# Batching the value products of a fused attention and MLP-mixer kernel: three eT tiles, two e tiles, one place for queries and keys

## The chip, the core and the metric

The kernel runs on one core of one Trainium2 chip. The metric is the device time of one execution in microseconds (us). The kernel before takes 1402.13 us, the median of three runs that lie between 1402.13 and 1402.17 us. One further execution was recorded by the hardware profiler; its span, from the first to the last instruction, is 1401.9 us, and all views below are of that execution.

Engines are named as in the profile: PE is the matrix engine (PEld its weight loads), DVE the vector engine, ACT the scalar engine, POOL the GpSimd engine, SP the engine whose queue issues most transfers. "L463" is line 463 of the kernel before.

## What is computed

```python
# q, k, v: (8, 8, 576, 64) float32; tau a scalar; the four weights arrive as float64
scores = (q @ k.T) / 8                         # per batch row and head, 576 x 576
thresh = scores.max(-1) - tau
scores = where(scores >= thresh, scores, -1e9)
attn   = softmax(scores)
x      = concat_heads(attn @ v)                # (8, 576, 512)

h   = relu(x.T @ w_tok1) @ w_tok2              # tokens are mixed: 576 -> 256 -> 576
u   = x + h.T
out = u + relu(u @ w_ch1) @ w_ch2              # channels are mixed: 512 -> 1536 -> 512
```

Everything is float32 on the chip. The weights are float64 in memory; they are loaded as pairs of 32-bit words and turned into float32 by integer and float operations on DVE, ACT and POOL, spread over the first units of the kernel.

## The kernel before

The attention is cut into 144 units, 18 for each of the eight batch rows (b = 0 to 7). A unit is 128 queries of two heads against all 576 keys. Nine units serve two pairs of heads: four blocks of the first pair, one shared block (`"s"`, the last 64 queries of both pairs), and four blocks of the second. The main loop does, for each unit `u`: the score products of `u`, the softmax normalization of `u-1`, the transposition of the weights of `u-2`, and the exponentials of `u`. Between these it slips in steps of the MLP of the batch row before, taken from the queue `todo` by `fill`; this filler is most of the PE work. At the end of the unit come the value products (`values`) that are due.

```python
LAG = 2
for u in range(len(units) + LAG + 4):
    ...
    scores(u)
    norm(u - 1)
    if b_now: weight(2)                  # steps of the conversion of the weights
    turn_blocks(u - LAG)                 # row b=0: turn(), with transposes on PE
    # when a group is complete: due += [(u + 2, ...)]  (u + 1 in row b=0)
    if b_now: fill(0.4)
    weight(2 if b_now else 1)
    weigh(u)
    if b_now: fill(0.6)
    weight(2 if b_now else 1)
    if t < 8: load_qk(n + 2 + t // 4, ..., t % 4)      # a quarter of a pair's q and k
    if t == 2: prep(n + 1)               # DVE transposes q and k, the loaded tiles are free again
    if t == 7: prep(n + 2)
    # while due: values(b, p, c); after the last group of a row: push(b)
```

A PE score product writes two PSUM tiles (`sc`, one per head). DVE takes the maxima, POOL makes a bias of them, and ACT writes `e` from `sc` (L316), which frees the PSUM tiles, and then takes the exponentials in place (L319):

```python
def scores(u):                            # cut
    sc = [(ps_3rd if b == 0 and (2 * u + h) % 3 == 2 else ps_sc).tile(...) for h in range(2)]   # ps_sc: two tiles
    nc.tensor.matmul(sc[h][rows, f, 0:HS], lhsT=qT[r, cols], rhs=kT[r, HS * f : HS * f + HS], ...)    # L301
    nc.vector.tensor_reduce(out=mx[:, c], in_=sc[h][:, :, 0:HS], axis=AX.XY, op=ALU.max)              # L306
    nc.gpsimd.tensor_scalar(out=bias[:, c], in0=mx[:, c], ...)                                        # L307

def weigh(u):
    e = work.tile([P, 2 * S], F32, tag="e", bufs=3, name=f"e_{u}")
    for h in range(2):                                                                               # L316
        nc.scalar.activation(out=eh, in_=sc[h][:, :, 0:HS], func=AF.Prelu, bias=bias[:, h : h + 1], ...)
    for h in range(2):                                                                               # L319
        nc.scalar.activation(out=eh, in_=eh, func=AF.Exp, bias=ntau, accum_out=rs[:, h : h + 1])
```

From row b=1 on, `e` is transposed in 32 x 32 blocks by DVE into `T` (L363), and 16 transfers from the SP queue (L373) put the blocks of a finished group in their places in `eT`. In row b=0 PE transposes `e` in three thirds, each into a PSUM tile of the pool `ps_tr` (two tiles), from which DVE or ACT copies it into `eT` (L352, L354):

```python
def turn_blocks(u):                       # cut; u here is two units back
    nc.vector.transpose(out=T..., in_=e...)                               # L363
    if place == n - 1:                    # the group is complete
        eTs[key] = work.tile([P, NK * 2 * P], F32, tag="eT", ...)         # two eT tiles
        for a in range(4):
            for i in range(4):
                nc.sync.dma_start(out=eTs[key][...], in_=T[...])          # L373
```

`values` multiplies one group (256 queries of one pair, or 64 of the shared block) with v. It uses one `ps_tr` tile, and ACT copies the result out (L413):

```python
def values(b, p, c):                      # cut
    ps = ps_tr.tile([P, MAIN], F32, tag="tr", name=f"pv_{b}_{p}_{c}")[:, 0:N]
    # 2 matmuls on vl (L403), 8 on lv (L408), two heads side by side in the PE columns
    nc.scalar.copy(out=x, in_=ps)         # L413
```

The filler consists of `turn_x` (L425), `tok1` (L434, ACT applies the relu), `tok2` (L441, DVE adds the result to xT, L445), `ch1` (L463, ACT applies the relu, L464) and `ch2` (L475 and L479, DVE copies the result, L484). All but `turn_x` use the two PSUM tiles of `ps_mm`. `push(b)` refills the queue when the attention of row b is done, three units into the next row, and sets how much filler a unit gets:

```python
KEEP = 45.0
def push(b):
    steps, old = token_mlp(b), list(todo)          # 5 turn_x, 2 tok1, 8 tok2
    todo.clear()
    for i in range(max(len(steps), len(old))):     # old and new steps in turn
        todo.extend(old[i : i + 1]); todo.extend(steps[i : i + 1])
    for i in ...: todo.extend(channel_mlp(b - b % 2, uT, i))
    quota = (sum(c for c, _ in todo) - (KEEP if b else 0.0)) / (UB - 1)     # UB = 18
```

Of the kernel before, what the change touches and what calls it, by code (L numbers as in the profile page):

```python
# [9 lines left out]
F32 = mybir.dt.float32  # L10
# [7 lines left out]
P = 128  # L18
# [3 lines left out]
def kernel(  # L22
# [26 lines left out]
    nc = tc.nc  # L49
    B, H, S, D = q.shape  # L50
# [7 lines left out]
    NT = NI + 1  # L58
    MT = [P] * NI + [LAST]
    NP = H // 2  # L60
    NTK = DTOK // P
# [3 lines left out]
    NK = 2 * S // P  # L65
# [4 lines left out]
    ld = ctx.enter_context(tc.tile_pool(name="ld", bufs=2))  # L70
    work = ctx.enter_context(tc.tile_pool(name="work", bufs=2))
# [11 lines left out]
    pairs = [(b, p) for b in range(B) for p in range(NP)]  # L83
# [3 lines left out]
    UB = 9 * NP // 2  # L87
# [5 lines left out]
    loaded = {}  # L93
    VL = 4
    vlast = [const.tile([P, P], F32, name=f"vl{i}") for i in range(VL)]

    def load_qk(n, eng, part=None):


        b, p = pairs[n]  # L100
        if n not in loaded:
            loaded[n] = [ld.tile([P, S // 32, 32], F32, tag=tag, name=f"{tag}_{n}") for tag in ("lq", "lk")]
        for i in range(4) if part is None else (part,):
            h, c = divmod(i, 2)
            for src, t, on in zip((q, k), loaded[n], eng):
                on.dma_start(
                    out=t[32 * i : 32 * i + 32], in_=src[b, 2 * p + h, :, 32 * c : 32 * c + 32].rearrange("(n t) d -> t n d", t=32)
                )

    def load_v(n):  # L110

        b, p = pairs[n]
        lv = ld.tile([P, NK, D], F32, tag="lv", bufs=4, name=f"lv_{n}")
        nc.sync.dma_start(out=lv, in_=v[b].rearrange("h s d -> (h s) d")[2 * S * p : 2 * S * p + 2 * S, :].rearrange("(c p) d -> p c d", p=P))
        vals[n] = lv
# [51 lines left out]
    def load_piece(i):  # L167
        if i >= len(pieces):
            return
        dst, src = pieces[i]  # L170
        rows = dst.shape[0]
        n = 1
        for d in dst.shape[1:]:
            n *= d
        raw = raw_at[i % NRAW][0:rows, 0 : n * (2 if wide(i) else 1)].bitcast(src.dtype)
        nc.sync.dma_start(out=like(raw, dst), in_=src)
        if wide(i):
            words = raw.bitcast(U32).rearrange("p (n w) -> p n w", w=2)
            h2 = work.tile([P, WMAX], F32, tag="o", name=f"h2_{i}")[0:rows, 0:n]
            raws[i] = like(words[:, :, 0], dst), like(words[:, :, 1], dst), like(h2, dst)  # L180
        else:
            raws[i] = like(raw, dst)
# [56 lines left out]
        weight(3 * i + 4 - steps_done)  # L239

    load_piece(0)
    load_qk(1, (nc.sync, nc.sync))
    load_v(0)
    for i in range(1, NRAW):
        load_piece(i)
# [26 lines left out]
    eTs = {}  # L272
    Ts = {}

    def in_blocks(b):
        return b > 0

    def prep(n):
        lq, lk = loaded.pop(n)
        made = []  # L280
        for src, name in ((lq, "qT"), (lk, "kT")):
            sb = work.tile([P, S], F32, tag=name, name=f"{name}_{n}")
            nc.vector.transpose(out=sb, in_=src.rearrange("p n d -> p (n d)"))
            made.append(sb)
        heads[n] = made
# [24 lines left out]
    def weigh(u):  # L310
        sc, bias = st.pop(u)
        rs = small.tile([P, 2], F32, tag="rs", name=f"rs_{u}")
        e = work.tile([P, 2 * S], F32, tag="e", bufs=3, name=f"e_{u}")
        for h in range(2):
            eh = e[:, S * h : S * h + S].rearrange("p (f x) -> p f x", f=2)
            nc.scalar.activation(out=eh, in_=sc[h][:, :, 0:HS], func=AF.Prelu, bias=bias[:, h : h + 1], scale=SCALE, alpha=STEEP)  # L316
        for h in range(2):
            eh = e[:, S * h : S * h + S]
            nc.scalar.activation(out=eh, in_=eh, func=AF.Exp, bias=ntau, accum_out=rs[:, h : h + 1])  # L319
        st[u] = e, rs  # L320
# [11 lines left out]
    def group_of(u):  # L332

        b, p0, t = units[u]
        if t == SHARED:
            return (b, p0, "s"), 0, 1
        i, c = divmod(t - (t > SHARED), NI)
        return (b, p0 + i, c // 2), c % 2, 2

    def turn(u, third):  # L340

        key, place, n = group_of(u)
        e = st[u]
        if third == 0 and place == 0:
            eTs[key] = work.tile([P, NK * 2 * P], F32, tag="eT", name=f"eT_{u}")
        if third == 2:
            st.pop(u)
        eT = eTs[key][:, 0 : NK * n * P].rearrange("p (c x) -> p c x", c=NK)
        ps = ps_tr.tile([P, MAIN], F32, tag="tr", name=f"tr{third}_{u}")[:, 0 : 3 * P].rearrange("p (c x) -> p c x", c=3)
        for c in range(3):  # L350
            k0 = (3 * third + c) * P
            nc.tensor.transpose(out=ps[:, c, :], in_=e[:, k0 : k0 + P], identity=ident)  # L352
        on = nc.scalar.copy if third == 1 and u % 2 else nc.vector.tensor_copy
        on(out=eT[:, 3 * third : 3 * third + 3, P * place : P * place + P], in_=ps)  # L354

    def turn_blocks(u):

        key, place, n = group_of(u)
        e = st.pop(u)
        if place == 0:  # L360
            Ts[key] = work.tile([P, NK * 2 * P], F32, tag="T", name=f"T_{u}")
        T = Ts[key][:, 0 : NK * n * P]
        nc.vector.transpose(  # L363
            out=T.rearrange("p (a c n x) -> p c a n x", a=4, c=NK, n=n)[:, :, :, place, :],
            in_=e.rearrange("p (c a x) -> p c a x", c=NK, a=4),
        )
        if place == n - 1:
            del Ts[key]
            eTs[key] = work.tile([P, NK * 2 * P], F32, tag="eT", name=f"eT_{u}")
            w = NK * n * 32  # L370
            for a in range(4):
                for i in range(4):
                    nc.sync.dma_start(  # L373
                        out=eTs[key][32 * a : 32 * a + 32, w * i : w * i + w], in_=T[32 * i : 32 * i + 32, w * a : w * a + w]
                    )
# [116 lines left out]


    KEEP = 45.0
    todo = deque()
    quota = 0.0
    credit = 0.0
# [11 lines left out]
    def push(b):  # L509
        nonlocal quota  # L510
        uT = xTs[b]
        steps, old = token_mlp(b), list(todo)
        todo.clear()
        for i in range(max(len(steps), len(old))):
            todo.extend(old[i : i + 1])
            todo.extend(steps[i : i + 1])
        for i in range(2) if b % 2 == 0 else range(2, (2 * S + GR - 1) // GR):
            todo.extend(channel_mlp(b - b % 2, uT, i))
        quota = (sum(c for c, _ in todo) - (KEEP if b else 0.0)) / (UB - 1)

    prep(0)
    due = deque()
    b_now = 0
    LAG = 2
    for u in range(len(units) + LAG + 4):
        on = u < len(units)
        if u == UB:
            late.close()
            ps_mm = ctx.enter_context(tc.tile_pool(name="ps_mm", bufs=2, space=bass.MemoryType.PSUM))
        if on:  # L530
            b_now, p0, t = units[u]
            n = b_now * NP + p0
        w = u - LAG
        back = 0 <= w < len(units)
        if on:
            scores(u)
        if 0 < u <= len(units):
            norm(u - 1)
        if b_now:
            weight(2)  # L540
        if back:
            key, place, many = group_of(w)
            if in_blocks(key[0]):
                turn_blocks(w)
            else:
                for i in range(3):
                    turn(w, i)
            if place == many - 1:
                b, p, c = key
                if c == 0 and p % 2 == 0:  # L550
                    split_middle(b * NP + p)
                if c == "s":
                    split_middle(b * NP + p + 1)
                when = u + (2 if in_blocks(b) else 1)
                due += [(when, b, p + i, c) for i in range(2 if c == "s" else 1)]
        if b_now:
            fill(0.4)
        weight(2 if b_now else 1)
        if on:
            weigh(u)  # L560
        if b_now:
            fill(0.6)
        weight(2 if b_now else 1)
        if on:
            m = n + 2 + t // 4
            if t < 8 and m < len(pairs):
                load_qk(m, (nc.scalar if b_now else nc.sync,) * 2, t % 4)
                if t % 4 == 3:
                    load_v(m)
            if t == 2:  # L570
                prep(n + 1)
            if t == 7 and n + 2 < len(pairs):
                prep(n + 2)
        while due and due[0][0] <= u:
            _, b, p, c = due.popleft()
            values(b, p, c)
            if p == NP - 1 and c == 1:
                push(b)
    need(len(pieces) - 1)
    quota = 1e9  # L580
# [29 lines left out]
```

## The time and the profile before

| what | value |
| --- | --- |
| median time of three runs | 1402.13 us |
| span of the profiled execution | 1401.9 us |
| DVE busy | 585.6 us (42%) |
| ACT busy | 589.1 us (42%) |
| POOL busy | 359.1 us (26%) |
| score products L301, x1280 | 192.3 us |
| value products L403 and L408, x1920 | 200.2 us |
| ch1 L463, x1920 | 401.7 us |
| ch2 L479, x864 | 388.9 us |
| transposes T on DVE, L363, x126 | 1369 ns each |
| first e operation on ACT, L316, x288 | 740 ns each |

The page gives for every engine how long it was busy, and a strip that cuts the span into 40 equal slices with one digit each: the busy share in tenths. The strip PEclk gives the granted clock of PE in the same slices. Groups of instructions are given by line, with the mean duration of one. In the timeline view a row is a run of equal instructions: its start, its length, the engine, the line, output and input, and, in brackets, how long the engine had been idle before it and which engine's work ended that idle time. PE's durations overlap a little, because a matmul's reported end is modelled; a start minus the start before it is the safer measure. The value row of the table is the sum of four groups (127.0, 43.6, 19.6 and 10.0 us).

### The profile page before, as it was taken

What the parts mean: (1) busy time and instruction counts of PE and PEld (TensorE: products, weight loads), DVE (VectorE), ACT (ScalarE), POOL (GpSimd) and SP (SyncE); (2) the same over time, 40 slices, a digit from 0 to 9 for tenths busy, and PEclk for the clock granted to TensorE, in tenths of its full rate; (3) what the DMA queues carried; (4) which work ended last, traced back from release to release, by engine and by line L of the source; (5) the groups of instructions that cost most, each with busy time, mean ns of one, the idle gap of its engine ahead of it and who ended that gap; (6) DMA issues with size and microseconds to landing.
All of it is one profiled execution on the core that took longest, in us unless ns stands there. A gap on an engine that the chain in (4) does not pass through costs nothing.

```text
span 1401.9 us, 19510 instructions
## 1 busy us (share of the span) xinstructions
PE 1332.0 (95%) x6866; PEld 833.3 (59%) x6866; DVE 585.6 (42%) x1009; ACT 589.1 (42%) x1328; POOL 359.1 (26%) x683
## 2 busy tenths in 40 slices
PE   5776899989999999999999999999999999999998
PEld 3443566646665567565656566565657566576675
DVE  5689674445444443434333444434333444201000
ACT  5676564444545444453334444443334444220110
POOL 4466462222222222212122222222212222100000
PEclk9998999989999999999999999999999999999999
DMA  6344654443444444443334444343343433300000
GB/s 127 92 109 116 170 141 111 96 120 90 115 125 112 106 94 97 101 96 92 87 97 92 100 94 104 94 107 80 96 96 80 104 90 82 86 8 16 8 8 23
DMA packets 257376, 128.34 MB, mean 92 GB/s; under 512 B 208064, under 2 KB 221376, under 8 KB 257280
## 3 DMA queue, kind: packets, MB, share of 16 engines
q1 hardware_dynamic: 131632, 111.46, 30.3%
q10 hardware_dynamic: 125648, 15.64, 7.0%
q8 instruction: 55, 0.90, 0.3%
q14 instruction: 41, 0.34, 0.1%
HBM read 43.25 MB, written 9.44 MB: 38 GB/s over the span
## 4 chain that ended last, share of the span: by engine, by line
PE 83%; DVE 7%; SPq 3%; ACT 2%; DMA 2%; POOL 1%; issue 1%; DVEq 0%; ACTq 0%; POOLq 0%
PE c L479 27%; PE c L463 24%; PE sc L301 11%; PE pv L408 7%; PE t L434 4%; PE t L441 3%; DVE mx L306 3%; PE pv L403 2%; SPq L373 2%; DVE T L363 2%; PE tx L425 1%; PE c L475 1%; PE pv_s L408 1%; DMA scratch<-in_moe_w_ch_dram 1%; ACT e L316 1%
## 5 line engine op out<-in xcount | busy, mean ns | idle before, releaser
L306 DVE TENSOR_REDUCE mx<-sc 128x1 f32<-128x576 f32 x288 | 204.7, 752 | 530.6 <-PE sc L301 528.8
L463 PE MATMUL c<-xT,wc 128*128 128x256 f32 (+1 forms) x1920 | 401.7, 362 | 4.1 <-ACT g L464 2.0
L479 PE MATMUL c<-wc,g 128*128 128x512 f32 x864 | 388.9, 596 | 0.0
L463 PEld LDWEIGHTS c<-xT,wc 128*128 128x128 f32 x1920 | 332.8, 190 | 75.2 <-issue 27.2
L307 POOL TENSOR_SCALAR bias<-mx,toff 128x1 f32<-128x1 f32 x288 | 80.1, 278 | 824.0 <-DVE mx L306 768.1
L479 PEld LDWEIGHTS c<-wc,g 128*128 128x128 f32 x864 | 157.8, 190 | 177.8 <-issue 176.3
L316 ACT ACTIVATE e<-sc,bias 128x576 f32<-128x576 f32 x288 | 199.0, 740 | 145.5 <-POOL bias L307 142.9
L464 ACT ACTIVATE g<-c 128x256 f32<-128x256 f32 (+1 forms) x240 | 86.6, 363 | 347.9 <-PE c L463 332.5
L329 POOL TENSOR_SCALAR e<-e,rr 128x576 f32<-128x576 f32 x288 | 219.3, 774 | 16.2 <-DVE rr L326 4.0
L319 ACT ACTIVATE e<-e,ntau 128x576 f32<-128x576 f32 x288 | 220.2, 773 | 0.0
L301 PE MATMUL sc<-kT,qT 64*128 64x288 f32 (+1 forms) x1280 | 192.3, 439 | 18.6 <-ACT e L316 9.7
L363 DVE STREAM_TRANSPOSE T<-e 128x1152 f32<-128x1152 f32 x126 | 172.5, 1369 | 15.7 <-DMA eT<-T 8.4
L301 PEld LDWEIGHTS sc<-kT,qT 64*128 64x128 f32 (+1 forms) x1280 | 104.5, 181 | 95.8 <-issue 47.7
L408 PE MATMUL pv<-eT,lv 128*64 128x256 f32 x1024 | 127.0, 392 | 0.0
L408 PEld LDWEIGHTS pv<-eT,lv 128*64 128x64 f32 x1024 | 76.6, 142 | 40.0 <-issue 5.4
L413 ACT COPY xT<-pv 128x256 f32<-128x256 f32 x64 | 23.8, 372 | 172.2 <-PE pv L408 155.1
L484 DVE COPY o<-c 128x512 f32<-128x512 f32 x36 | 24.4, 678 | 164.6 <-PE c L479 164.6
L441 PE MATMUL t<-w,a 128*128 128x288 f32 x256 | 76.2, 426 | 12.2 <-DVE xT L445 10.1
L434 PE MATMUL t<-x_sb,w 128*128 128x512 f32 x160 | 73.4, 606 | 0.0
L441 PEld LDWEIGHTS t<-w,a 128*128 128x128 f32 x256 | 46.4, 194 | 35.9 <-DVE xT L445 15.2
L445 DVE TENSOR_TENSOR xT<-xT,t 128x288 f32<-128x288 f32 x64 | 28.0, 441 | 76.8 <-PE t L441 76.7
L319 ACT ACTIVATION_READ_ACCUMULATOR e<-e,ntau 128x1 f32 x288 | 57.1, 198 | 0.0
(48 smaller groups left out, 605.2 us busy)
## 6 DMA issues: line engine op xcount, KB each, us to landing
eT<-T SPq DMA_DIRECT2D x896, 72.0 KB, 2.1
scratch<-in_moe_w_ch_dram SPq DMA_DIRECT2D x24, 512.0 KB, 4.0
lv<-in_v_dram SPq DMA_DIRECT2D x32, 288.0 KB, 3.5
out_dram<-o SPq DMA_DIRECT2D x36, 256.0 KB, 2.2
eT<-T SPq DMA_DIRECT2D x224, 36.0 KB, 1.9
lk<-in_k_dram ACTq DMA_DIRECT2D x108, 72.0 KB, 2.8
lq<-in_q_dram ACTq DMA_DIRECT2D x104, 72.0 KB, 2.1
lq<-in_q_dram SPq DMA_DIRECT2D x24, 72.0 KB, 3.5
```

What stands on the lines that cost most here:

```text
L301: nc.tensor.matmul(sc[h][rows, f, 0:HS], lhsT=qT[r, cols], rhs=kT[r, HS * f : HS * f + HS], start=True, stop=True)
L306: nc.vector.tensor_reduce(out=mx[:, c], in_=sc[h][:, :, 0:HS], axis=AX.XY, op=ALU.max)
L316: nc.scalar.activation(out=eh, in_=sc[h][:, :, 0:HS], func=AF.Prelu, bias=bias[:, h : h + 1], scale=SCALE, alpha=STEEP)
L319: nc.scalar.activation(out=eh, in_=eh, func=AF.Exp, bias=ntau, accum_out=rs[:, h : h + 1])
L329: nc.gpsimd.tensor_scalar(out=eh, in0=eh, scalar1=rr[:, h : h + 1], scalar2=1.0, op0=ALU.mult, op1=ALU.mult)
L363: nc.vector.transpose(out=T.rearrange("p (a c n x) -> p c a n x", a=4, c=NK, n=n)[:, :, :, place, :], in_=e.rearrange("p (c a x) -> p c a ...
L408: nc.tensor.matmul(to[r], lhsT=lv[:, j, :], rhs=eT[:, j], start=False, stop=(c == NI - 1), skip_group_check=True)
L434: nc.tensor.matmul(ps, lhsT=w1[:, t, P * m : P * m + P], rhs=x_sb[:, t, :], start=(t == 0), stop=(t == NT - 1))
L441: nc.tensor.matmul(ps, lhsT=s["a"][:, m, P * c : P * c + P], rhs=w2[:, m, HS * f : HS * f + HS], start=(m == 0), stop=(m == NTK - 1))
L463: nc.tensor.matmul(ps, lhsT=wc1[:, j, c, :], rhs=uT[:, c, GR * i : GR * i + n], start=(c == 0), stop=(c == NCC - 1))
L464: nc.scalar.activation(out=s["g"][:, j, 0:n], in_=ps, func=AF.Relu)
L479: nc.tensor.matmul(flat, lhsT=s["g"][:, j, P * t : P * t + P], rhs=wc2[:, j, :], start=False, stop=(j == NJ - 1), skip_group_check=True)
```

## The change

The change alters five things.

1. **Two groups of values per visit.** From row b=1 on, a finished group is not multiplied on its own. It is held in a list until a visit takes several: of the five groups of nine units, the first two go together, the shared block (a call for each of the two pairs) goes with the third, and the last goes alone. The purpose is to switch PE less often between the shapes of the value products and the others.
2. **Three eT tiles** instead of two, since groups now wait longer; this costs 9 KiB of memory per partition.
3. **Two e tiles instead of three, and one place for queries and keys** (`lq` and `lk` with one buffer each instead of two), which pay for it. The loads of queries and keys move: eight pieces for each pair, issued in the units in which the one place is free.
4. **A reserve in row b=1** (the second row): `KEEP_FIRST = 20.0` keeps 20 us of filler back, for the units between the end of the queue and the next `push`.
5. **Token steps further apart**: ahead of the first `tok1` and of the first `tok2` two old steps are put instead of one.

```diff
--- before.py
+++ after.py
@@ -94,18 +94,19 @@
     VL = 4
     vlast = [const.tile([P, P], F32, name=f"vl{i}") for i in range(VL)]
 
-    def load_qk(n, eng, part=None):
+    def load_qk(n, eng, parts=range(8)):
 
 
         b, p = pairs[n]
         if n not in loaded:
-            loaded[n] = [ld.tile([P, S // 32, 32], F32, tag=tag, name=f"{tag}_{n}") for tag in ("lq", "lk")]
-        for i in range(4) if part is None else (part,):
+            loaded[n] = [ld.tile([P, S // 32, 32], F32, tag=tag, bufs=1, name=f"{tag}_{n}") for tag in ("lq", "lk")]
+        for part in parts:
+            i, which = divmod(part, 2)
             h, c = divmod(i, 2)
-            for src, t, on in zip((q, k), loaded[n], eng):
-                on.dma_start(
-                    out=t[32 * i : 32 * i + 32], in_=src[b, 2 * p + h, :, 32 * c : 32 * c + 32].rearrange("(n t) d -> t n d", t=32)
-                )
+            eng[which].dma_start(
+                out=loaded[n][which][32 * i : 32 * i + 32],
+                in_=(q, k)[which][b, 2 * p + h, :, 32 * c : 32 * c + 32].rearrange("(n t) d -> t n d", t=32),
+            )
 
     def load_v(n):
 
@@ -239,7 +240,6 @@
         weight(3 * i + 4 - steps_done)
 
     load_piece(0)
-    load_qk(1, (nc.sync, nc.sync))
     load_v(0)
     for i in range(1, NRAW):
         load_piece(i)
@@ -310,7 +310,7 @@
     def weigh(u):
         sc, bias = st.pop(u)
         rs = small.tile([P, 2], F32, tag="rs", name=f"rs_{u}")
-        e = work.tile([P, 2 * S], F32, tag="e", bufs=3, name=f"e_{u}")
+        e = work.tile([P, 2 * S], F32, tag="e", name=f"e_{u}")
         for h in range(2):
             eh = e[:, S * h : S * h + S].rearrange("p (f x) -> p f x", f=2)
             nc.scalar.activation(out=eh, in_=sc[h][:, :, 0:HS], func=AF.Prelu, bias=bias[:, h : h + 1], scale=SCALE, alpha=STEEP)
@@ -342,7 +342,7 @@
         key, place, n = group_of(u)
         e = st[u]
         if third == 0 and place == 0:
-            eTs[key] = work.tile([P, NK * 2 * P], F32, tag="eT", name=f"eT_{u}")
+            eTs[key] = work.tile([P, NK * 2 * P], F32, tag="eT", bufs=3, name=f"eT_{u}")
         if third == 2:
             st.pop(u)
         eT = eTs[key][:, 0 : NK * n * P].rearrange("p (c x) -> p c x", c=NK)
@@ -366,7 +366,7 @@
         )
         if place == n - 1:
             del Ts[key]
-            eTs[key] = work.tile([P, NK * 2 * P], F32, tag="eT", name=f"eT_{u}")
+            eTs[key] = work.tile([P, NK * 2 * P], F32, tag="eT", bufs=3, name=f"eT_{u}")
             w = NK * n * 32
             for a in range(4):
                 for i in range(4):
@@ -492,6 +492,7 @@
 
 
     KEEP = 45.0
+    KEEP_FIRST = 20.0
     todo = deque()
     quota = 0.0
     credit = 0.0
@@ -511,15 +512,19 @@
         uT = xTs[b]
         steps, old = token_mlp(b), list(todo)
         todo.clear()
-        for i in range(max(len(steps), len(old))):
-            todo.extend(old[i : i + 1])
-            todo.extend(steps[i : i + 1])
+
+        for i, step in enumerate(steps):
+            n = 2 if i in (NT, NT + NTK) else 1
+            todo.extend(old[:n] + [step])
+            del old[:n]
+        todo.extend(old)
         for i in range(2) if b % 2 == 0 else range(2, (2 * S + GR - 1) // GR):
             todo.extend(channel_mlp(b - b % 2, uT, i))
-        quota = (sum(c for c, _ in todo) - (KEEP if b else 0.0)) / (UB - 1)
+        quota = (sum(c for c, _ in todo) - (KEEP if b else KEEP_FIRST)) / (UB - 1)
 
     prep(0)
     due = deque()
+    held = []
     b_now = 0
     LAG = 2
     for u in range(len(units) + LAG + 4):
@@ -551,8 +556,15 @@
                     split_middle(b * NP + p)
                 if c == "s":
                     split_middle(b * NP + p + 1)
-                when = u + (2 if in_blocks(b) else 1)
-                due += [(when, b, p + i, c) for i in range(2 if c == "s" else 1)]
+                group = [(b, p + i, c) for i in range(2 if c == "s" else 1)]
+                if in_blocks(b):
+
+                    held += group
+                    if (p % 2, c) in ((0, 1), (1, 0), (1, 1)):
+                        due += [(u + 2,) + g for g in held]
+                        held.clear()
+                else:
+                    due += [(u + 1,) + g for g in group]
         if b_now:
             fill(0.4)
         weight(2 if b_now else 1)
@@ -562,11 +574,17 @@
             fill(0.6)
         weight(2 if b_now else 1)
         if on:
-            m = n + 2 + t // 4
-            if t < 8 and m < len(pairs):
-                load_qk(m, (nc.scalar if b_now else nc.sync,) * 2, t % 4)
-                if t % 4 == 3:
-                    load_v(m)
+
+
+            when = {3: (2, 0, 2), 4: (2, 2, 4), 5: (2, 4, 6), 6: (2, 6, 8), 8: (3, 0, 3), 0: (1, 3, 6), 1: (1, 6, 8)}
+            if u == 0:
+                load_qk(1, (nc.sync, nc.sync), range(0, 3))
+            if t in when:
+                m, lo, hi = when[t]
+                if n + m < len(pairs):
+                    load_qk(n + m, (nc.scalar if b_now else nc.sync,) * 2, range(lo, hi))
+            if t in (3, 7) and n + 2 + t // 4 < len(pairs):
+                load_v(n + 2 + t // 4)
             if t == 2:
                 prep(n + 1)
             if t == 7 and n + 2 < len(pairs):
```

## The prediction

> **What bounds the kernel now.** I read the busy line and the two strips of the page first.
>
> ```profile
> PE 1332.0 (95%) x6866; PEld 833.3 (59%) x6866; DVE 585.6 (42%) x1009; ACT 589.1 (42%) x1328; POOL 359.1 (26%) x683
> ...
> PE   5776899989999999999999999999999999999998
> ...
> PEclk9998999989999999999999999999999999999999
> ```
>
> PE is the bound, but not everywhere: the first five slices (175 us) are at 5 to 8 tenths, and slice 9 (280 to 315 us) dips in PE and in clock. The table by stages says it in numbers.
>
> ```profile
> 9.00:95.00 86.00, 66.77 (x428) 41.32 (x430) 64.14 (x135) 60.87 (x132) 45.44 (x78) 0.94 0.45 103
> 104.00:206.40 102.40, 82.42 (x413) 52.57 (x412) 81.92 (x126) 61.88 (x130) 61.40 (x67) 0.92 0.56 150
> 290.90:303.60 12.70, 8.58 (x38) 4.56 (x36) 7.18 (x12) 6.21 (x13) 4.42 (x10) 0.65 0.55 136
> 420.00:1250.00 830.00, 821.92 (x4309) 512.63 (x4308) 324.09 (x546) 346.01 (x794) 187.61 (x396) 1.00 0.39 93
> ```
>
> The columns are length, busy PE, PEld, DVE, ACT and POOL, clock, DMA share, GB/s. From 420 us PE idles 8 of 830 us: there only PE's own work and its changeovers count. In b=0 (9 to 95) and while weights are converted (104 to 206) DVE is as busy as PE, and chains of waits decide.
>
> Third, the timeline of a quiet unit, for the slack between a unit's stages.
>
> ```profile
> 857.38 1.24 PE L301 MATMUL sc<-kT,qT 64*128 64x288 f32 x8
> ...
> 858.65 1.42 DVE L306 TENSOR_REDUCE mx<-sc 128x1 f32<-128x576 f32 x2 [5.89 <-PE sc L301]
> ...
> 860.58 1.38 DVE L363 STREAM_TRANSPOSE T<-e 128x1152 f32<-128x1152 f32 x1 [0.23 <-DMA eT<-T]
> 860.86 1.37 ACT L316 ACTIVATE e<-sc,bias 128x576 f32<-128x576 f32 x2
> ...
> 863.92 1.24 PE L301 MATMUL sc<-kT,qT 64*128 64x288 f32 x8
> ```
>
> L316 frees the score tiles at 862.2; the next scores start at 863.9, 6.5 us after the last. L316 starts before T (of two units back) ends at 861.96: with three e tiles it need not wait for it.
>
> Fourth, the same for PE around the dip.
>
> ```profile
> 290.88 1.24 PE L301 MATMUL sc<-kT,qT 64*128 64x288 f32 x8
> 294.10 2.95 PE L301 MATMUL sc<-kT,qT 64*128 64x288 f32 x8 [1.98 <-ACT e L316]
> 299.18 1.12 PE L403 MATMUL pv<-eT,vl 128*64 128x256 f32 x4 [2.14 <-DMA eT<-T]
> 300.06 3.65 PE L408 MATMUL pv<-eT,lv 128*64 128x256 f32 x16
> ```
>
> Two units without filler: PE waits, and equal blocks then take twice as long (L408 3.65 against 1.90 us).
>
> **What the Trainium skill says.** "TensorEngine Tiling (Array Packing)", Key Properties: a change of tiling mode drains PE. The trace agrees: filler to filler costs about 0.0 to 0.1 us, and a unit "scores, filler" takes 0.44 us more than its matmuls (median of 31), one with a value visit 0.63 us (43). "TensorE: Matmul & The Clock Gate", Part 1, says an idle PE falls to half clock; the 0.65 above agrees. "PSUM — Partial Sum Buffer", Engine vs sequencer instructions, says ACT and DVE run strictly in order; the trace shows no overtaking, so whatever holds L316 also holds the relus behind it.
>
> **The change part by part.** Nominal PE time of a unit is the sum of its matmuls in the program order of each kernel, with 213 ns for 256 columns (L463 x8 from 614.63 to 616.46, less a changeover).
>
> *Value visits.* After unit 20 they fall from 68 to 41: 27 x (0.63 - 0.44) = 27 x 0.19 = **-5.1 us**. All matmuls stay.
>
> *Three groups in one visit.* The shared block's two and the next group need three `ps_tr` tiles; there are two. The third waits for ACT's L413 of the first, which stands behind L319 and relus. With ch1 filler ACT is done about 8.2 us into the unit; PE is there at 6.1 (unit 28) or 7.7 (46 and 55), and I charge 2.0 + 2 x 0.8 = **+3.6 us**. With ch2 filler, drained by DVE, I expect nothing.
>
> *Two e tiles, b=1 on.* L316 of unit u waits for T of u-2. T ends 4.3 to 4.6 us after the unit's scores start (scores 1.27, L306 1.42, the reciprocal 0.33, T 1.38); then L316 1.37. So scores follow scores after 5.9 us at the least, where unit 47 took 4.8 without a wait. In the new order few units are shorter, nominal plus 0.45: unit 33 (4.9), 53 (5.7), 63 (3.1: a chunk of filler came early). That is 1.0 + 0.2 + 2.8 = **+4.0 us**. Relus behind the later L319 free `ps_mm` later by 0.8 to 1.1 us; the slack there is about as large, so **+1.0 us** in all.
>
> *Two e tiles, b=0.* Here PE reads e. L316 of unit 8 started at 57.18; the last transposes of unit 6 run at 58.23 and end at 58.78, so L316 moves by 1.6 us. In the odd unit behind it ACT's eT copy (60.80) then stands behind the later L319 and starts at 62.2; the third transposes (61.33) and the next scores follow 0.9 to 1.4 us late. The even unit is unharmed, as DVE's copy is its limit. Eight odd units x 0.9 = **+7 us**. Nothing behind absorbs it: the weight conversion is tied to the units.
>
> *Queries and keys.* The same number of loads. The last piece of a pair is issued one unit before `prep`; a unit mostly lasts 4 us or more, landing takes 2.1 to 3.5 (the page's DMA issues): **0**.
>
> *Reserve.* 20 us of filler leave b=1 for b=2. Units 38 to 43 took 11.3 us more than nominal plus changeovers (2.1, 6.1, -0.8, 0.1, 2.0, 1.8). In the new order units 38 and 39 have filler; unit 40 is short (0.9 to 1.3), and the eight tok2 still come back to back in units 44 and 45, each waiting some 2 us for DVE's L445 behind T. Left 5.7: **-5.6 us**. The price: in units 22 to 27 PE waits for DVE's conversion anyway, and filler taken from there opens gaps. Units 22 to 24 hold 7.3 us less and get some 6.2 us shorter; with 26 and 27, less 26's old wait for weights, I charge **+1 us**.
>
> *Token steps.* Idle time before tok1 and tok2 from 420 us on is a few us, mostly tok2 behind L445, which this doesn't touch: **-1 us**.
>
> Sum: -5.1 + 3.6 + 4.0 + 1.0 + 7 - 5.6 + 1 - 1 = +4.9, so **1407 us**.
>
> **The rivals.** (a) *The e wait is hidden.* ACT is 42% busy, and scores follow scores after 6.5 us or more nearly everywhere. If b=0 has slack that I overlook (its chain of waits passes through DVE and PE more than ACT), the +7 goes, and the third group may find its tile free: 1402 - 5.1 - 5.6 + 4 = about 1395. Against it: in the new program order 197 of the 288 L316 wait for DVE or PE as well, where all waited for POOL alone. (b) *DVE's weight conversion becomes the bound of b=1.* DVE is busy 82 of 102 us there; if PE stands in all units 22 to 27, the reserve's price is 6 to 9 us: 1412 to 1415. For it: the intervals of 8 to 14 us there. (c) *`prep` waits for late loads*, as one place leaves a single unit between issue and use, and SP's queue also waits for weight buffers: 1 us for each of some 30 pairs would give 1435. Against it: the landing times above, and from b=1 on these loads are on ACT's own queue.
>
> **Range and chances.** The terms of b=0 (0 to 10) and of the conversion (-2 to +8) carry most of the spread; the visits' 5 us are firm. I take 1393 to 1420. Two per cent are 28 us, beyond all but (c): 0.01 faster, 0.96 within 2%, 0.03 slower.
>
> **What the new profile would show.** The visits: units with two groups 0.19 us cheaper in all. The e tiles: L316 waiting for DVE T and, before 100 us, for PE tr; the first unit of b=1 starts near 111 instead of 104 us. The third group: L403 waiting for ACT xT. The reserve: no dip in PE or clock near 300 us, more idle PE between 150 and 206. Unit 63: a wait of almost 3 us for ACT before scores. I am wrong if b=0 isn't longer, if PE idles at `prep` for queries and keys, or if the third group waits in every row.

## The result and the profile after

The changed kernel takes **1436.13 us**, the median of five runs (1435.1 to 1440.9), against 1402.13: the ratio is 1.0253, its 95% interval 1.0237 to 1.0268. It is slower, by 34 us, and outside the predicted range of 1393 to 1420.

The page of the kernel after, busy line and the two strips:

```profile
PE 1350.7 (94%) x6866; PEld 845.9 (59%) x6866; DVE 585.2 (41%) x1009; ACT 585.3 (41%) x1328; POOL 354.0 (25%) x683
...
PE   7877799999999989999999889999999989999998
...
PEclk9897999999999999999999999999999999999999
```

The work of DVE, ACT and POOL is about what it was. The dip of slice 9 is gone, but the PE strip has new 8s in slices 15, 23, 24 and 33, in a part that was all 9s. Two rows of the table by stages, with the columns of the table before, and three more where the 8s are:

```profile
290.90:303.60 12.70, 11.63 (x65) 5.80 (x64) 4.39 (x8) 6.05 (x14) 2.99 (x7) 1.00 0.54 130
420.00:1250.00 830.00, 801.86 (x4168) 500.15 (x4166) 322.59 (x544) 334.41 (x776) 185.09 (x394) 0.99 0.38 92
483.00:528.00 45.00, 37.69 (x247) 26.58 (x250) 16.60 (x30) 15.29 (x40) 8.38 (x18) 0.92 0.33 75
817.00:864.00 47.00, 39.04 (x250) 26.68 (x252) 16.60 (x30) 17.03 (x44) 8.38 (x18) 0.93 0.35 81
1150.00:1198.00 48.00, 40.04 (x255) 27.07 (x257) 16.60 (x30) 17.29 (x45) 8.38 (x18) 0.93 0.33 78
```

From 420 to 1250 us PE idled 8 us before and idles 28 now, and of those 28 us 23 lie in the last three rows (7.3, 8.0 and 8.0), where the clock is also down to 0.92 or 0.93. These are units 63 to 66, 99 to 102 and 135 to 138: the token steps of batch rows 2, 4 and 6, which PE works off while the attention of rows 3, 5 and 7 runs. The starts of units in the traces say the same. The third column is the first experiment, the kernel after with the third e tile given back:

| start of unit (us) | before | after | after, three e tiles |
| --- | --- | --- | --- |
| 18 (row b=1 begins) | 104.0 | 103.6 | 101.2 |
| 38 | 290.9 | 280.3 | 273.1 |
| 56 | 424.0 | 423.9 | 414.3 |
| 63 | 480.9 | 483.1 | 472.3 |
| 67 | 517.9 | 527.8 | 509.9 |
| 99 | 806.0 | 817.7 | 799.1 |
| 103 | 842.0 | 863.5 | 841.0 |
| 135 | 1129.9 | 1150.9 | 1127.3 |
| 139 | 1165.9 | 1197.4 | 1169.2 |
| span | 1401.9 | 1434.1 | 1404.9 |

After is level with before at unit 56. It then falls back in four units at a time: 7.7 us from 63 to 67, 9.8 from 99 to 103, 10.5 from 135 to 139. Between them it loses little (2.2 us from 56 to 63, 1.8 from 67 to 99, nothing from 103 to 135).

What happens there is read from unit 99 in the timeline of the kernel after:

```profile
814.05 1.36 DVE L363 STREAM_TRANSPOSE T<-e 128x1152 f32<-128x1152 f32 x1
...
814.30 1.46 POOL L329 TENSOR_SCALAR e<-e,rr 128x576 f32<-128x576 f32 x2
...
815.52 1.37 ACT L316 ACTIVATE e<-sc,bias 128x576 f32<-128x576 f32 x2 [3.87 <-DVE T L363]
...
817.71 1.24 PE L301 MATMUL sc<-kT,qT 64*128 64x288 f32 x8
...
818.88 2.05 PE L463 MATMUL c<-xT,wc 128*128 128x128 f32 x16
...
820.92 1.38 DVE L363 STREAM_TRANSPOSE T<-e 128x1152 f32<-128x1152 f32 x1 [0.23 <-DMA lk<-in_k_dram]
822.41 1.37 ACT L316 ACTIVATE e<-sc,bias 128x576 f32<-128x576 f32 x2 [3.36 <-POOL e L329]
...
825.19 0.43 ACT L464 ACTIVATE g<-c 128x128 f32<-128x128 f32 x2
...
825.51 2.29 PE L441 MATMUL t<-w,a 128*128 128x288 f32 x4 [4.57 <-ACT g L464]
...
827.59 1.91 PE L463 MATMUL c<-xT,wc 128*128 128x128 f32 x8
```

T ends at 822.30 and L316 starts at 822.41. The bracket names POOL's L329 because that ended at 822.34, a moment after T; the unit before shows which of the two counts: there L316 starts at 815.52, just behind T (815.41), while L329 runs until 815.76. Behind L316 stand both L319, and only then come the relus L464 of the two ch1 steps (818.88, x16). Both `ps_mm` tiles are held by those steps, so PE stands for 4.57 us, until 825.51. After that its clock is halved for some 5 us: the four L441 take 2.29 us, one group of eight L463 1.91 us; in the next unit, from 831.0 us on, the same blocks take 1.24 and 1.05.

The list of waits of the kernel after (sum, count, longest):

```profile
ACT e L316 <- POOL e L329: 142.8, 45, 7.0
ACT e L316 <- DVE T L363: 130.0, 50, 5.5
...
PE sc L301 <- ACT e L316: 10.3, 12, 2.3
...
PE t L441 <- ACT g L464: 9.9, 4, 4.6
```

The first two are ACT's idle time, which costs nothing by itself. What counts is where PE waits for ACT: the scores L301 for L316, and tok2 (L441) for a relu.

### The profile page after: what moved, and what is told of

The parts are those of the page before. It is cut to its first block, busy times and chain, and to the rows that moved or that the text cites. A ratio compares the mean times of both kernels' runs of the same rounds, so it can differ in the third digit from the quotient of the medians.

```text
span 1434.1 us, 19760 instructions
## 1 busy us (share of the span) xinstructions
PE 1350.7 (94%) x6866; PEld 845.9 (59%) x6866; DVE 585.2 (41%) x1009; ACT 585.3 (41%) x1328; POOL 354.0 (25%) x683
## 4 chain that ended last, share of the span: by engine, by line
PE 76%; DVE 9%; ACT 5%; DMA 3%; SPq 2%; issue 2%; POOL 1%; ACTq 0%; DVEq 0%; POOLq 0%
PE c L479 24%; PE c L463 20%; PE sc L301 10%; PE pv L408 8%; PE t L434 4%; DVE mx L306 4%; PE t L441 4%; DVE T L363 3%; PE pv L403 2%; ACT e L316 2%; SPq L373 2%; ACT e L319 2%; DMA eT<-T 2%; PE c L475 1%; PE tx L425 1%
## 5 line engine op out<-in xcount | busy, mean ns | idle before, releaser
L463 PE MATMUL c<-xT,wc 128*128 128x256 f32 (+1 forms) x1920 | 402.1, 363 | 7.4 <-DVE xT L445 3.7
L463 PEld LDWEIGHTS c<-xT,wc 128*128 128x128 f32 x1920 | 336.5, 192 | 80.4 <-issue 21.9
L316 ACT ACTIVATE e<-sc,bias 128x576 f32<-128x576 f32 x288 | 197.4, 737 | 304.2 <-POOL e L329 142.8
L301 PE MATMUL sc<-kT,qT 64*128 64x288 f32 (+1 forms) x1280 | 204.5, 441 | 17.5 <-ACT e L316 10.3
L329 POOL TENSOR_SCALAR e<-e,rr 128x576 f32<-128x576 f32 x288 | 216.7, 765 | 17.1 <-ACT g L464 3.2
L319 ACT ACTIVATE e<-e,ntau 128x576 f32<-128x576 f32 x288 | 220.0, 772 | 0.0
L464 ACT ACTIVATE g<-c 128x256 f32<-128x256 f32 (+1 forms) x240 | 83.1, 361 | 307.5 <-PE c L463 294.2
L301 PEld LDWEIGHTS sc<-kT,qT 64*128 64x128 f32 (+1 forms) x1280 | 111.7, 182 | 107.5 <-issue 34.7
L441 PE MATMUL t<-w,a 128*128 128x288 f32 x256 | 82.0, 451 | 23.6 <-DVE xT L445 13.7
L441 PEld LDWEIGHTS t<-w,a 128*128 128x128 f32 x256 | 48.4, 204 | 52.7 <-DVE xT L445 22.0
L413 ACT COPY xT<-pv 128x256 f32<-128x256 f32 x64 | 23.6, 371 | 108.4 <-PE pv L408 102.6
L445 DVE TENSOR_TENSOR xT<-xT,t 128x288 f32<-128x288 f32 x64 | 28.0, 441 | 97.3 <-PE t L441 97.2
L319 ACT ACTIVATION_READ_ACCUMULATOR e<-e,ntau 128x1 f32 x288 | 56.8, 197 | 0.0
```

The lines of the kernel that those rows point to most:

```text
L329: nc.gpsimd.tensor_scalar(out=eh, in0=eh, scalar1=rr[:, h : h + 1], scalar2=1.0, op0=ALU.mult, op1=ALU.mult)
L441: nc.tensor.matmul(ps, lhsT=s["a"][:, m, P * c : P * c + P], rhs=w2[:, m, HS * f : HS * f + HS], start=(m == 0), stop=(m == NTK - 1))
L463: nc.tensor.matmul(ps, lhsT=wc1[:, j, c, :], rhs=uT[:, c, GR * i : GR * i + n], start=(c == 0), stop=(c == NCC - 1))
L464: nc.scalar.activation(out=s["g"][:, j, 0:n], in_=ps, func=AF.Relu)
```

## The experiments

A median is compared with runs of the kernel before on the same chip (1402.4 us for experiments 1 to 4, 1401.3 for 5 to 8, 1401.0 for 9 to 12); so where runs of two of these groups are set against each other, 1 us or so means nothing. "Theory" and a number or letter are those of the expectations.

**1. The third e tile given back to the kernel after.** The small tiles go from six to five copies each to make room.

```diff
-    e = work.tile([P, 2 * S], F32, tag="e", name=f"e_{u}")
+    e = work.tile([P, 2 * S], F32, tag="e", bufs=3, name=f"e_{u}")
```

> The changed kernel with three e tiles again (the small tiles go from six to five places, to make room). Theory 1 (two e tiles and the two old steps ahead of tok2 act together: L316 waits for T, the relus of two ch1 steps stand behind it, both ps_mm tiles stay full, PE waits): the waits of units 63 to 66, 99 to 102 and 135 to 138 fall from some 11 us a row to 2 to 5, and the time to 1402 to 1414 us. Theory 2 (the two old steps alone): no change, 1430 to 1436 us. Theory 3 (two groups per visit, or one place for queries and keys): no change either.

Measured: **1410.18** (1406.69 to 1412.86), ratio 1.0058 (1.0036 to 1.0080): 26 of the 34 us are gone. In its timeline unit 99 reads:

```profile
799.07 1.24 PE L301 MATMUL sc<-kT,qT 64*128 64x288 f32 x8
...
801.49 1.41 ACT L316 ACTIVATE e<-sc,bias 128x576 f32<-128x576 f32 x2 [1.72 <-POOL bias L307]
...
802.28 1.38 DVE L363 STREAM_TRANSPOSE T<-e 128x1152 f32<-128x1152 f32 x1 [0.24 <-DMA eT<-T]
...
804.31 0.42 ACT L464 ACTIVATE g<-c 128x128 f32<-128x128 f32 x2
...
804.62 2.05 PE L441 MATMUL t<-w,a 128*128 128x288 f32 x4 [2.33 <-ACT g L464]
```

L316 starts before T. The relu comes 5.24 us behind the scores, where it came 7.48 us behind them, and PE's wait is 2.33 instead of 4.57 us. From unit 38 to 139 the two traces differ by 21 us: 15.6 in the three stretches named above, 4.8 in the units with `turn_x` (40 and 41, 59 and 60, 95 and 96, 131 and 132). Units 40, 59, 95 and 131 are short, 4.3 to 4.8 us with three tiles, and there the next scores wait for L316. In the kernel after, unit 60 begins so:

```profile
452.84 1.87 PE L301 MATMUL sc<-kT,qT 64*128 64x288 f32 x8 [0.31 <-ACT e L316]
```

Of these 20.4 us, 11.5 are longer waits of PE. In the rest PE counts as busy for longer: at half clock behind a wait, or, as here, in scores whose second head waits (1.87 us instead of 1.24).

**2. The old order of the token steps in the kernel after** (one old step between any two again).

```diff
-            n = 2 if i in (NT, NT + NTK) else 1
-            todo.extend(old[:n] + [step])
+            todo.extend(old[i : i + 1])          # and steps[i : i + 1] in turn
```

> The changed kernel with the token steps mixed as before, one old step ahead of each. Theory 1: unit 99 gets a relu ahead of L316 again, two ch1 steps no longer stand together ahead of tok2, and most of the 3 x 11 us goes: 1403 to 1412 us. Theory 4 (two e tiles alone are enough): it stays at 1425 to 1436 us. Theory 3: it stays at 1430 to 1436 us.

Measured: **1427.96** (1426.87 to 1429.7), 1.0187 (1.0171 to 1.0204): 8.2 us less than after, and longer than theory 1 allowed.

**3. Two e tiles alone, in the kernel before.**

```diff
-    e = work.tile([P, 2 * S], F32, tag="e", bufs=3, name=f"e_{u}")
+    e = work.tile([P, 2 * S], F32, tag="e", name=f"e_{u}")
```

> The kernel before with two e tiles and nothing else. Theory 1: L316 waits for T here too, but with the old mix of steps it costs only 4 to 10 us, 1406 to 1412 us. Theory 4 (two e tiles alone): 1425 us or more. Theory 2: 1402 to 1406 us.

Measured: **1420.13**, 1.0144 (1.0102 to 1.0186), in two pairs near 1414 and 1425. Two tiles alone cost some 18 us by the median (12 to 23 by the pairs), without any other part of the change. In its timeline the same token step:

```profile
810.35 1.24 PE L301 MATMUL sc<-kT,qT 64*128 64x288 f32 x8
...
811.52 1.16 PE L463 MATMUL c<-xT,wc 128*128 128x128 f32 x8
...
812.51 1.14 PE L441 MATMUL t<-w,a 128*128 128x288 f32 x4
812.72 0.28 ACT L464 ACTIVATE g<-c 128x128 f32<-128x128 f32 x1 [2.04 <-PE c L463]
...
813.55 1.38 DVE L363 STREAM_TRANSPOSE T<-e 128x1152 f32<-128x1152 f32 x1 [0.23 <-POOL bias L307]
...
815.03 1.37 ACT L316 ACTIVATE e<-sc,bias 128x576 f32<-128x576 f32 x2 [2.03 <-POOL e L329]
```

L316 waits for T (814.93) here too. But with one ch1 step between scores and tok2 its relu (812.72) stands ahead of L316, and PE has a free tile.

**4. Two old steps alone, in the kernel before** (the edit of 2, the other way).

> The kernel before with two old steps ahead of the first tok1 and the first tok2, and nothing else. Theory 1: with three e tiles the relus stand behind L319 only, 1402 to 1410 us. Theory 2 (the steps alone): 1425 us or more. Theory 4: 1401 to 1404 us.

Measured: **1406.74** (1405.67 to 1412.48), 1.0040 (1.0024 to 1.0055): +4.3 us. Theory 1, that neither part costs much without the other, falls: two e tiles cost some 18 us alone. What is left of it is a smaller share: the two steps are worth 8.2 us with two tiles (2 against after).

**5. T taken ahead of the scores.** If L316 waits for T because DVE comes to T only behind maxima and reciprocals of the newer unit, T first removes the wait with two tiles still in place.

```diff
+        if back and in_blocks(units[w][0]):
+            turn_blocks(w)               # w = u - LAG; no longer behind norm(u - 1)
         if on:
             scores(u)
```

> The changed kernel, two e tiles, but DVE does T of unit u-2 ahead of the maxima of unit u, so that no L316 waits for it from b=1 on; the two old steps stay. Theory A (L316 waits for T, and behind it scores and relus wait): nearly all that three e tiles brought comes back, 1406 to 1414 us, and in the waits ACT e L316 <- DVE T and <- POOL e are gone. Theory B (two tiles cost something else, such as the transposes of row b=0 or memory): 1430 us or more.

Measured: **1419.75** (1417.25 to 1421.77), 1.0127 (1.0110 to 1.0144): −16 us, less than theory A asked for. By the two traces it gains 27 us in rows 2 to 7 and loses 8 in row 1. From the waits of that kernel between 118 and 225 us, and then of the kernel after there:

```profile
ACT scratch L192 <- DMA scratch<-in_moe_w_ch_dram: 22.7, 6, 9.8
```

```profile
ACT scratch L192 <- DMA scratch<-in_moe_w_ch_dram: 6.5, 4, 2.7
```

The 16 transfers into eT now stand ahead of the weight loads in the SP queue, so the weights land later; with them ahead again (run 9) this sum is 9.1 us.

**6 and 7. The third group of a visit.** Run 6 is the kernel after with three e tiles and the old order of token steps; run 7 also gives the shared block a visit of its own. The number of visits is the same, none has more than two groups.

```diff
-                    if (p % 2, c) in ((0, 1), (1, 0), (1, 1)):
+                    if (p % 2, c) in ((0, 1), (1, 1)) or c == "s":
```

> The changed kernel with three e tiles and the old mix of token steps: what is left are the two groups per visit, the third eT tile, the one place for queries and keys and the reserve. By the sum of the prediction for these parts (visits -5.1, third group +3.6, reserve -5.6 + 1): 1393 to 1400 us. If the steps cost 4.3 us here as alone: 1406 us. If the visits or the single place cost too: 1408 us or more.

> As the one before, but the shared block's two calls are a visit of their own, so that no visit has more than two groups; the number of visits stays the same. If the third group's wait for its ps_tr tile is what the profile shows (2.4 us in unit 28, little elsewhere): 2 to 4 us less than the one before. If it is hidden: no difference.

Measured: **1408.63** (1406.28 to 1412.18), 1.0050 (1.0035 to 1.0066), and **1398.65** (1395.53 to 1401.3), 0.9982 (0.9971 to 0.9993). With three e tiles the token steps are worth only 1.6 us here, which the noise can hide; the edit of run 7 brings 10.0 us, where 2 to 4 were expected. Unit 28 in the timeline of the kernel of experiment 1, for the wait of the third group itself:

```profile
200.19 0.38 ACT L464 ACTIVATE g<-c 128x256 f32<-128x256 f32 x1
200.62 0.33 ACTq L106 DMA_DIRECT2D lq<-in_q_dram  x1
201.86 0.35 ACTq L106 DMA_DIRECT2D lk<-in_k_dram  x1
202.25 0.33 ACT L413 COPY xT<-pv_s 128x64 f32<-128x64 f32 x2 [1.68 <-DMA eT<-T]
...
202.52 0.65 PE L403 MATMUL pv<-eT,vl 128*64 128x256 f32 x4 [2.36 <-ACT xT L413]
```

PE waits for ACT's copy L413. ACT's last relu ends at 200.57, and the products to be copied ended before that. But two issues of loads of q and k stand ahead of the copy on ACT's queue, and the second goes only at 201.86. For 1.68 of PE's 2.36 us ACT is idle behind them. In the trace of run 6 the same gap is 2.1, 1.4 and 1.0 us in units 28, 46 and 55. So new loads and third group act together here; no run moves the loads alone, and what the second issue waits for isn't shown.

**8. The reserve alone, in the kernel before.**

```diff
-        quota = (sum(c for c, _ in todo) - (KEEP if b else 0.0)) / (UB - 1)
+        quota = (sum(c for c, _ in todo) - (KEEP if b else 20.0)) / (UB - 1)
```

> The kernel before with 20 us kept back in b=1 and nothing else. By the prediction's term, -5.6 + 1: 1396 to 1399 us. If the gaps opened in the units of the weight conversion take it back: 1401 to 1404 us.

Measured: **1395.96** (1393.65 to 1397.98), 0.9959 (0.9944 to 0.9974): −5.3 us. Its table by stages at the old dip (291 to 304 us) has PE busy for 12.76 of 13 us at full clock:

```profile
291.00:304.00 13.00, 12.76 (x67) 6.70 (x66) 6.26 (x9) 7.12 (x17) 3.73 (x7) 1.00 0.63 152
```

Runs 7 and 8 also weigh the visits. The kernel of 7 has the reserve, 41 visits instead of 68, and none of the other costs measured so far, and yet it is 2.7 us slower than that of 8. From unit 20 to 143 its trace is only 2.4 us shorter (1071.1 against 1073.5), where 5.1 were expected. In the quiet rows 4 and 6 it gains about what 0.19 us a visit makes (168.9 against 169.5 and 169.6 us); in rows 3, 5 and 7, with token steps, it loses. Unit 64, in the timelines of run 7 and then run 8:

```profile
478.55 0.41 DVE L445 TENSOR_TENSOR xT<-xT,t 128x288 f32<-128x288 f32 x1
...
479.01 1.24 PE L441 MATMUL t<-w,a 128*128 128x288 f32 x4 [1.34 <-DVE xT L445]
...
480.29 0.46 DVE L445 TENSOR_TENSOR xT<-xT,t 128x288 f32<-128x288 f32 x1 [1.33 <-PE t L441]
...
480.80 1.16 PE L463 MATMUL c<-xT,wc 128*128 128x128 f32 x8 [0.55 <-DVE xT L445]
```

```profile
482.17 1.24 PE L441 MATMUL t<-w,a 128*128 128x288 f32 x4 [0.37 <-ACT g L464]
482.68 0.42 DVE L445 TENSOR_TENSOR xT<-xT,t 128x288 f32<-128x288 f32 x1
...
483.25 1.06 PE L463 MATMUL c<-xT,wc 128*128 128x128 f32 x8
```

In one, tok2 and ch1 wait for tiles that DVE's L445 frees, late because it stands behind T; in the other a relu frees the tile that tok2 needs. Beyond its matmuls and changeovers unit 64 takes 2.6 us in run 7 and 0.1 in run 8; units 100 and 136 take 1.6 to 1.8 against about 0. That is some 5.8 us in three units, about what the visits were to save. That fewer visits must lead to these waits isn't shown: the filler falls on other units.

**9 to 12. T first from row 2 on**, so that the weight loads stay ahead in row 1 (`units[w][0] > 1` in the edit of 5): in the kernel after (9); in the kernel before with the reserve (10); in that of run 7 (11); in that of run 7 with two e tiles and six copies of the small tiles (12).

> The changed kernel, two e tiles and all else of it, with T ahead of the maxima from b=2 on only; b=0 and b=1 stay as in the changed kernel. The row sums of the run with T first everywhere were 26 us lower than the changed kernel's from b=2 on and 8 us higher in b=1, where the 16 eT transfers came ahead of weight loads in the SP queue. If that is right: 1407 to 1413 us. If the wait for T is not what two e tiles cost in b=2 to 7, but something of b=0: 1420 us or more.

> The kernel before with the reserve of 20 us and T ahead of the maxima from b=2 on; three e tiles. The wait of tok2 for DVE's addition, which stands behind T, gets shorter: some 0.5 to 1 us in two or three units a row, 1390 to 1394 us. If T ahead delays the maxima and with them L316: 1396 us or more.

> The changed kernel with three e tiles, the old mix of steps, no visit of three groups, and T ahead of the maxima from b=2 on. The kernel without the last took 1398.65 us; T first should bring about 5 us, as its rows did against those with three e tiles: 1391 to 1396 us.

> As the one before, but with two e tiles. From b=2 on no L316 waits for T, so the third tile should be worth nothing there; what is left is what two tiles cost in b=0 and b=1. If b=0 costs the 7 us of the prediction and b=1 some 3: 1400 to 1406 us. If b=0 hides it: 1392 to 1398 us.

| run | median (us) | ratio to before (95%) |
| --- | --- | --- |
| 9 after, T first | 1412.36 (1406.62 to 1416.36) | 1.0078 (1.0055 to 1.0102) |
| 10 before, reserve, T first | **1388.67** (1387.07 to 1389.29) | 0.9911 (0.9896 to 0.9925) |
| 11 run 7, T first | 1388.76 (1385.79 to 1393.15) | 0.9904 (0.9888 to 0.9920) |
| 12 run 11, two e tiles | 1397.92 (1393.41 to 1402.49) | 0.9975 (0.9962 to 0.9988) |

Unit 99 of run 9, with two e tiles:

```profile
809.94 1.38 DVE L363 STREAM_TRANSPOSE T<-e 128x1152 f32<-128x1152 f32 x1 [1.67 <-DMA eT<-T]
...
811.85 1.24 PE L301 MATMUL sc<-kT,qT 64*128 64x288 f32 x8
...
814.28 1.41 ACT L316 ACTIVATE e<-sc,bias 128x576 f32<-128x576 f32 x2 [1.72 <-DMA eT<-T]
...
817.10 0.42 ACT L464 ACTIVATE g<-c 128x128 f32<-128x128 f32 x2
...
817.41 1.24 PE L441 MATMUL t<-w,a 128*128 128x288 f32 x4 [2.33 <-ACT g L464]
```

T comes before the scores. The relu is back at 5.25 us behind the scores and PE's wait at 2.33, as with three tiles: T ahead of the scores does for this unit what the tile does. In all it brings 24 us to the kernel after. Of that, 9.9 are its gain where three tiles are there anyway (run 7 to 11), which leaves, as an estimate, some 14 for the e wait in rows 2 to 7. With T first two tiles still cost 9.2 us (run 12 to 11). Rows 0 and 1, where T comes as before, hold 4.2 of the 6.2 us between their two traces.

In row 0, first scores to unit 18, eight profiled executions with three e tiles took 91.1 to 96.4 us (mean 93.2), six with two 94.7 to 103.6 (98.5): about 5.3 us. The units say what it is made of. Units 9, 11, 13, 15 and 17 take 0.4 to 0.7 us longer in all six executions with two tiles (unit 11: 6.4 us instead of 5.9), except where they take far longer still. In four of the six, one to three of units 9 to 15 take 9.2 or 10.6 us at a clock of 0.52 to 0.63; with three tiles only unit 13 does so, in two of eight (8.3 us). The pairs of run 3, 11 us apart, may have this cause, but only one execution near 1414 us has a trace, and that has no such unit.

Runs 10 and 11 are the best of all, level with each other, and 0.9% faster than before. Run 10 is two small edits of the kernel before.

## Why the prediction was wrong, by its own steps

| term | predicted | measured |
| --- | --- | --- |
| two e tiles, b=1 on | +5.0 (4.0 + 1.0) | about +21 (after less 1, 26, less row 0) |
| two e tiles, b=0 | +7 | about +5 |
| three groups in a visit | +3.6 | +10.0 (6 less 7) |
| value visits | −5.1 | 0 to +3 (run 11 less 10, 7 less 8; with the loads and eT tiles that go with them) |
| reserve | −4.6 | −5.3 |
| token steps | −1 | +1.6 (1 less 6) |
| queries and keys | 0 | none at `prep`; a part of the +10.0 |

With the visits at 2.7 the last column adds up to 35 us, near the result of 34. It must: these are the steps of one chain of runs, from after by 1, 6, 7 and 8 to before. In another order they share out differently; the token steps cost 8.2 us while two e tiles are there, and 4.3 alone in the kernel before.

**The step that failed is "Two e tiles, b=1 on"**: +5.0 us were predicted, and about 21 measured. The dependence was right (L316 of u waits for T of u−2), and so was its size in the units I named: unit 63 lost 2.3 us (2.8 predicted) and unit 33 0.7 (1.0). My list of units too short for scores to follow scores left out 40, 59, 95 and 131, which with the units behind them lost 4.8 us. The larger part is the second half of the step. I put the relus down as 1.0 us, "the slack there is about as large"; with the halved clock they cost some 13 of the 21 us between units 38 and 139. I had taken the slack from quiet units. In the token-step units there is none: both `ps_mm` tiles hang on relus that stand behind L316 and two L319. There the relu came 2.2 us later and PE's wait grew from 2.33 to 4.57 us. I had myself cited the Trainium skill ("PSUM — Partial Sum Buffer", Engine vs sequencer instructions) for ACT and DVE working strictly in order, and unit 99 agrees; its consequence has to be followed to every instruction behind the one that waits, in every kind of unit.

**The clock was left out.** A wait of PE was priced at its length. In unit 99 of the kernel after, the halved clock adds about 2.4 us to the 4.57: 1.05 in L441, 0.86 in L463, 0.44 in the next scores (1.68 instead of 1.24). My fourth view had shown this (3.65 us instead of 1.90) and I didn't carry it into the sum.

**Third group.** It waits for L413, as predicted, and unit 28's 2.36 us are near the 2.0 charged. But I had L413 behind L319 and relus alone; the loads ahead of it on ACT's queue make up 1.68 us there. Of these I had asked only whether they reach `prep` in time. Between runs 6 and 7 unit 28 differs by 3.6 us, 46 and 55 together by 1.8, the other visits of three groups by 0.1 to 0.6 each, where I expected nothing or 0.8. Unit 64 differs by 2.0, but not by the third group: PE waits 1.34 and 0.55 us in both traces, and in that of run 6 the clock is halved behind these waits.

**Visits**, which I called firm, were not: the gain on PE is real only where no other wait sets the time, and tok2's wait for L445, which I had called untouched by the token steps, moved with the visits. **Token steps**: with two ch1 together ahead of tok2, both tiles wait for relus; terms that share a resource don't simply add. **Reserve**: right, and so was the view that the dip near 300 us goes.

**Row 0** came out near the predicted 7 us, but partly by luck. The chain of waits I named cost 0.4 to 0.7 us in five odd units, 2.6 us in all, instead of 0.9 in eight; what fills it up is mostly the halved clock, which I had not counted. The single trace of after shows unit 18 at 103.6, not 111: its first scores start at 7.2 instead of 8.9 us, and row 0 varies by some 5 us between executions with the same number of tiles.

**Rivals.** (a) falls. (b), DVE's conversion: it would have shown in run 8, which gains the whole 5.3 us. (c) gave 1435 us, close to the result, for a cause that isn't there: the scores' waits for prepared keys come down to one in the list, at the very start, and `prep` itself waits for a load once, for 1.3 us. What the loads do cost comes another way, ahead of L413. A rival whose number fits isn't thereby right.

```profile
PE sc L301 <- DVE kT L283: 7.2, 1, 7.2
```

## What to carry to other kernels

A buffer taken away is to be priced by what stands behind the waiting instruction on its engine: go through each stage in which that engine also frees PSUM tiles, not through a quiet unit. Before buffers are spent or saved, ask whether the last reader can come earlier: the third e tile was worth 26 us in the kernel after and 9 with T ahead of the scores (run 11, which also lacks the new token steps and the third groups). Where a reorder moves transfers, look at what else waits in the same queue, ahead and behind. And a wait of PE is to be priced with the halved clock that may follow it.

## What the runs showed of the hardware

A wait of 2.33 us of PE was followed by half speed in one execution and not in another: in unit 99 the four L441 behind it took 2.05 us in experiment 1 and 1.24, full speed, in run 9. By the traces it is a matter of where the wait falls. In all fourteen traces the halved clock begins and ends on a grid of 3.413 us and lasts one, two or three of its steps (57, 29 and 13 times; the last piece of each trace is cut off). Around unit 99, two steps of experiment 1 and then one of run 9, with the columns of the tables by stages:

```profile
801.50:804.90 3.40, 1.07 (x9) 0.88 (x8) 1.88 (x4) 3.24 (x8) 1.73 (x3) 1.00 0.58 142
804.90:808.32 3.42, 3.42 (x14) 2.66 (x13) 0.46 (x1) 0.00 (x0) 0.00 (x0) 0.50 0.44 108
```

```profile
815.47:818.88 3.41, 1.47 (x8) 1.26 (x9) 0.20 (x1) 2.05 (x7) 1.01 (x2) 1.00 0.00 0
```

In the first, the whole wait lies in one step, PE is busy for 31% of it, and the next step runs at half clock. In the second, the step before holds a part of the wait, PE is busy for 43%, and the clock stays. Taking all traces from 200 to 1380 us, 14 steps at full clock were followed by a halved one, and PE was busy for at most 45% in each; 4804 were not, and PE was busy for at least 43%. In rows 0 and 1 the bound is less sharp: there the clock was halved after one step with PE busy for 73%, and not after one with 42%. The Trainium skill ("TensorE: Matmul & The Clock Gate", Part 1) has the clock fall after an idle window of about 3.4 us and calls the window free-running. The grid agrees with the length and with free-running. An idle window need not be idle throughout, though: here it was enough that PE stood for more than half of it.
